# Low bits of float64 weights taken by a rounding on ScalarE, the sign as a halfword, one integer step per tile

## The chip, the core and the metric

The kernel runs on one core of a Trainium2 chip. Its engines work side by side, each through its own list of instructions in order: TensorE (PE in the profile, its weight loads PEld), VectorE (DVE), ScalarE (ACT), GpSimd (POOL), and SyncE (SP), which issues the transfers. The metric is the device time of one execution in microseconds, lower is better.

## What is computed

Three blocks follow each other: an attention with a pooled and a local part, a dense feed-forward block, and a block with eight experts. The change touches only how the weights of the middle block are made.

```python
h = x @ w_in                                   # x: 2304 x 512, w_in: 512 x 2048
g = np.where(pos, h, np.where(neg, 0.0, (h + beta) ** 2 / (4.0 * beta)))
return g @ w_out                               # w_out: 2048 x 512
```

`w_in` and `w_out` are float64. On the chip each double is two 32-bit words, the low word `lw` (even places) and the high word `hw` (odd places). To make a float32 of it, the kernel needs the sign, the exponent moved to float32's range, the 20 mantissa bits of `hw` moved up by three, and the three top bits of `lw` behind them.

## The kernel before

**Tiles.** `w_in` and `w_out` come as 16 tiles each of 128 x 512 doubles: 32 tiles, numbered by `f` (0 to 15) and `w` (1 for `w_in`, 0 for `w_out`). `feed` loads them in pairs into `RAW[w, f]` (named raw in the profile).

**One tile.** `prep(w, f)` takes a tile: `scale64` has ScalarE write `t = hw * 2^-111` read as float32 (`t<-raw`; in the first tiles the buffer is called gar), and then has GpSimd write `hw * 0` over `hw`, which leaves a signed zero (`raw<-raw`, POOL). VectorE then does two integer steps: `hw |= lw >> 29` (`raw<-raw`, DVE) and `t = (t << 3) | hw` (`t<-t,raw`). `parts` splits the result in a high part, a copy to fp32r on ScalarE (`wi<-t` or `wo<-t`), and a low part, the difference `t - hi`, on VectorE or GpSimd (also `wi<-t,wi` or `wo<-t,wo`). Tiles of `w_out` are also transposed on TensorE and multiplied with the gate's weights (`gate_rows`). A tile lands over the place of its raw form.

**Around it.** The first part of the program mixes four things: the attention of 16 pairs of heads (`pooled`, `local`), the 32 tiles, the load of its output in chunks of 256 rows (`load_chunks`, xio and xts), and the feed-forward block. That last one goes in steps: one step is 12 matmuls `xts,wi` (`gemm1`), a gate on ScalarE, VectorE and GpSimd (`gates`, gar, ghi, glo), and matmuls `wo,ghi` and `wo,glo`. There are 7 chunks of 16 steps, 112 in all, and the first 32 go through the two first chunks. A tile of number f is wanted by step f of the first chunk, so the first 32 steps follow the tiles. Until the first step TensorE fills its idle time with matmuls of an identity (`bk<-cst`).

**Order.** The program writes the order of every engine itself when it is built: each piece of work is a generator, `run` always takes the piece that could start first, with priorities (`PRIO`), and `spend` keeps the assumed time of each engine. A generator that yields a dict of two engines is put on that which would finish it first (`SUB` are the prices for the low part). So a change of one piece reorders everything beside it. The temporaries `TT` (`temps` holds the free ones) allow two tiles in work, and four early on. Line 128 issues all of ScalarE's work, line 141 that of VectorE and GpSimd, lines 120 and 124 that of TensorE, line 106 the transfers.

Of the kernel before, what the change touches and what calls it, by code (L numbers as in the profile page):

```python
# [11 lines left out]
F32 = mybir.dt.float32  # L12
F32R = mybir.dt.float32r
BF = mybir.dt.bfloat16
I32 = mybir.dt.int32
AF = mybir.ActivationFunctionType
OP = mybir.AluOpType
# [27 lines left out]
AI, AJ, AK = (-1,1,-1)  # L45
BACK = dict(V=0.0, G=1250.0, A=500.0)
SUB = (1600.0,1250.0)
DL = (300.0,2000.0)
RA, RB = (2,3)
GF = 565.0  # L50
# [42 lines left out]
def body(ctx, tc, qk_d, v4_d, vw_d, win, wout, wg, w1, w2, cst_d, bits_d, out):  # L93
# [4 lines left out]
    def spend(e, ns):  # L98

        at = max(free[e], cur[0] + (0.0 if cur[1] == e == "P" else 130.0 if cur[1] == e else 250.0))  # L100
        free[e] = cur[0] = at + ns
        cur[1] = e

    def dma(out, x):

        nc.sync.dma_start(out, x)  # L106
        free["D"] = max(free["D"], cur[0] + DL[0]) + 4.0 * int(np.prod(out.shape)) / 360.0
        return free["D"] + DL[1] - cur[0]

    def size(x):  # L110
        return int(np.prod(x.shape[1:]))
# [14 lines left out]
    def act(out, x, f, **kw):  # L126
        spend("A", {AF.Exp: 280.0, AF.Relu: 145.0}.get(f, 85.0) + 0.83 * size(x))
        return nc.scalar.activation(out, x, f, **kw)  # L128
# [15 lines left out]
    V = Engine("V", nc.vector, 65.0, 1.05)  # L144
    G = Engine("G", nc.gpsimd, 100.0, 2.3)
    ctx.enter_context(tc.manual_schedule())
    P = ctx.enter_context(tc.tile_pool(name="fixed", bufs=1))
# [17 lines left out]
    def f32(x):  # L165
        return x.bitcast(F32)
# [4 lines left out]
    WI, WO, RAW = {}, {}, {}  # L171

    def place(w, f, dt, name):
        return P.tile([128, 1024 if w else 1040], dt, name=nm(name), tag=f"w{w}_{f}", bufs=1)
# [3 lines left out]

    L = P.tile([128, NT, E], F32, name="L")
    w2g = P.tile([128, 16, 2, E], F32R, name="w2g")  # L180
    halfs = P.tile([128, 2], F32, name="halves")
    half, mhalf = halfs[:, 0:1], halfs[:, 1:2]
    V.memset(half, 0.5)
    V.memset(mhalf, -0.5)

# [3 lines left out]
    def words(w, f):  # L191
        return (RAW[w, f].rearrange("p (a b) -> p a b", b=2)[:, :, i] for i in range(2))
# [19 lines left out]
    def put(gen, at, e="N", got=None, last=""):  # L212
        seq[0] += 1
        late = RP if gen.__name__ in ("route", "index") and gen.gi_frame.f_locals["r"] == 1 else 0
        i = gen.gi_frame.f_locals.get("i", 9) if gen.__name__ in ("pooled", "local", "vsum") else 0
        queue[e].append((PRIO.get(gen.__name__, 2) + late + (0 if not i and gen.__name__ not in ("pooled", "local", "vsum") else (AK if gen.gi_frame.f_locals.get("g") else AI) if i < 4 else 0 if i < 8 else AJ), at, seq[0], gen, got, last))

    def spawn(gen, e="N", delay=0.0):
        put(gen, cur[0] + delay, e)
# [49 lines left out]
    def done(*k):  # L269
        return k[1] < 0 or k in flags  # L270

    def mark(*k):
        flags[k] = cur[0]
# [4 lines left out]
    def need(e, *names, cond=None, bank=0, temp=0):  # L278

        def f():  # L280
            few = [n for n in temps if n < (temp() if callable(temp) else temp)]
            if (cond and not cond()) or any(not room[n] for n in names) or len(open_banks()) < bank or (temp and not few):
                return None
            got = open_banks()
            got = got[:bank] if B0 else got[::-1][:bank]
            for b in got:
                banks.remove(b)
            return (got if bank > 1 else got[0] if bank else None, temps.pop(temps.index(max(few))) if temp else None,
                    *[room[n].pop(0) for n in names])
        f.engine = e  # L290
        return f
# [43 lines left out]
    def arrived(*k):  # L335
        mark(*k)
        yield "N"
# [17 lines left out]
    def feed():  # L355
        for j in range(16):
            for w in (1, 0):
                RAW[w, j] = place(w, j, I32, "raw")[:, 0:1024]
                n = dma(RAW[w, j], (win[:, j, :] if w else wout[j]).bitcast(I32))
                spawn(arrived("raw", j, w), "N", n)  # L360
# [140 lines left out]
    def scale64(w, f, t):  # L501
        _, hw = words(w, f)
        yield "A"
        act(t, f32(hw), AF.Copy, scale=2.0 ** -111)
        yield "G"
        G.tensor_scalar(f32(hw), f32(hw), 0.0, 1.0, op0=OP.mult, op1=OP.mult)
        mark("scaled", f, w)
        yield "N"

    def parts(w, f, x, n):  # L510
        (WI if w else WO)[f] = to = place(w, f, F32R, "wi" if w else "wo").rearrange("p (s c) -> p s c", s=2)
        hi, lo = (to[:, i, 0:512] for i in range(2))
        act(hi, x, AF.Copy)
        e = yield {"V": SUB[0], "G": SUB[1]}
        (G if e == "G" else V).tensor_tensor(lo, x, f32(hi), OP.subtract)
        mark("parts", f, w)
        if w:
            temps.append(n)
            mark("prep", f, 1)

    def prep(w, f):
        _, n = yield need("V", temp=lambda: 2 + MORE * (not done("av", FX, 0)), cond=lambda: done("raw", f, w) and done("begun", f - 1, w))
        mark("begun", f, w)
        t = TT[n]
        spawn(scale64(w, f, t))
        yield need("V", cond=lambda: done("scaled", f, w))
        ti = t.bitcast(I32)
        lw, hw = words(w, f)

        V.scalar_tensor_tensor(hw, lw, 29, hw, op0=OP.logical_shift_right, op1=OP.bitwise_or)  # L530
        V.scalar_tensor_tensor(ti, ti, 3, hw, op0=OP.logical_shift_left, op1=OP.bitwise_or)
        spawn(parts(w, f, t, n), "A")
        if w:
            return
        spawn(gate_rows(f, t))
        yield need("N", cond=lambda: done("parts", f, 0) and done("turned_rows", f))
        temps.append(n)
        mark("prep", f, 0)

    def gate_rows(f, x):  # L540

        b, _ = yield need("P", bank=1)
        ps = bank(b)
        for k in range(4):
            transpose(ps[:, 128 * k:128 * k + 128], x[:, 128 * k:128 * k + 128], ident)
        mark("turned_rows", f)
        _, _, kr = yield need("A", "rows")
        rows = at([128, 512], F32, f"rows{kr}")
        act(rows, ps, AF.Copy)
        drop(bank=b)  # L550
        b, _ = yield need("P", bank=1)
        pg = bank(b)[:, 0:E]
        for k in range(4):
            mm(pg, rows[:, 128 * k:128 * k + 128], wgk[:, k], start=k == 0, stop=k == 3)
        drop(rows=kr)
        yield need("A", cond=lambda: f in WO)

        to = WO[f][:, :, 512:520], w2g[:, f]
        for x in to:
            act(x[:, 0], pg, AF.Copy)  # L560
        yield "V"
        for x in to:
            V.tensor_tensor(x[:, 1], pg, f32(x[:, 0]), OP.subtract)
        drop(bank=b)
        mark("w2g", f)

    lw = []
# [238 lines left out]
    for f in range(16):  # L806
        put(prep(1, f), 0.0)
        put(prep(0, f), 0.0)
# [37 lines left out]

    cb = rt([128, 384], BF, "cb")
    tri_bf, low_bf, ones_bf = (cb[:, 128 * i:128 * i + 128] for i in range(3))
# [6 lines left out]
    V.memset(ones_bf, 1.0)  # L855
    bits = rt([128, NIT, 31], I32, "bits")
    dma(bits, bits_d)
# [3 lines left out]
    V.memset(openm, 1.0)  # L861
    first = rt([1, E], BF, "first")
    V.tensor_scalar(first, cst[0:1, C_E:C_E + E], 1.0 / 16, None, op0=OP.mult)
    tp = rt([128, NT, 2], BF, "tp")
    V.tensor_copy(tp[:, :, 0], cst[:, C_P:C_P + 1].to_broadcast([128, NT]))
    V.tensor_copy(tp[:, :, 1], cst[:, C_T:C_T + NT])
    low = rt([128, NT, 32], BF, "low")
    V.memset(low, 0.0)
# [6 lines left out]
    def kept(at, *shape):  # L875
        n = int(np.prod(shape))
        x = keep[:, at:at + n]
        return x if len(shape) == 1 else x.rearrange("p (a b) -> p a b", b=shape[1])
# [19 lines left out]
    def route(r):  # L898
        m = kept(18 * (r % 2), NT)
        bases = [keep[:, 36 + i:37 + i].bitcast(I32) for i in range(2)]  # L900
        V.tensor_reduce(m, L, AX.X, OP.max)
        Ah = rt([128, NT, E], BF, "A")
        oh = kept(90 + 8 * (r % 2), E)
        base = None
        for it, (sh, nj) in enumerate(STEPS if r < E - 1 else ()):
            if it == 0:
                thr = bits[:, 0, 0:nj]
            else:
                thr = rt([128, 31], I32, "thr", 1)[:, 0:nj]
                V.tensor_tensor(thr, pre, ni.to_broadcast([128, nj]), OP.bitwise_xor)  # L910
            C = rt([128, NT, 31], BF, "C", 1)
            V.tensor_tensor(C[:, :, 0:nj], m[:, :, None].to_broadcast([128, NT, nj]),
# [445 lines left out]
```

## Time and profile before

| what | us |
|---|---|
| median of 3 runs | 899.41 (894.22 to 908.81) |
| the profiled execution: device time | 900.66 |
| its span, first to last instruction | 898.5 |
| busy in the span: PE / DVE / ACT / POOL | 858.7 / 514.9 / 463.1 / 439.2 |
| first matmul of the first step | 61.8 |
| last issue of a weight tile's integer steps | 204.7 |

In the rows below, a stretch is given in us from the span's start. A row of the grouped view names line, engine, operation, out<-in, the shape of output and input, how many there are, the busy time in us and the mean in ns of one, and behind the second bar the idle time of the engine just ahead of them, with what ended it. Busy time of PE is no measure of its load, since its matmuls overlap.

### The profile page before, as it was taken

What the parts mean: (1) busy time and instruction counts of PE and PEld (TensorE: products, weight loads), DVE (VectorE), ACT (ScalarE), POOL (GpSimd) and SP (SyncE); (2) the same over time, 40 slices, a digit from 0 to 9 for tenths busy, and PEclk for the clock granted to TensorE, in tenths of its full rate; (3) what the DMA queues carried; (4) which work ended last, traced back from release to release, by engine and by line L of the source; (5) the groups of instructions that cost most, each with busy time, mean ns of one, the idle gap of its engine ahead of it and who ended that gap; (6) DMA issues with size and microseconds to landing.
All of it is one profiled execution on the core that took longest, in us unless ns stands there. A gap on an engine that the chain in (4) does not pass through costs nothing.

```text
span 898.5 us, 20588 instructions
## 1 busy us (share of the span) xinstructions
PE 858.7 (96%) x7891; PEld 777.8 (87%) x7891; DVE 514.9 (57%) x1469; ACT 463.1 (52%) x1295; POOL 439.2 (49%) x498
## 2 busy tenths in 40 slices
PE   7879999989899999999999999998999999999995
PEld 6768888878899999999999877777988998989995
DVE  6788989876454543423221564475576766767520
ACT  5877786776466666544444551032343443544641
POOL 3765477654244544444444210033855756657741
PEclk9999999999899999999999999997999999999998
DMA  9755455223222310301000000053433544436620
GB/s 308 232 176 185 139 179 194 88 61 111 89 64 70 103 42 15 95 1 49 1 25 1 30 1 6 1 207 126 145 122 128 183 140 152 150 101 209 208 84 27
DMA packets 39010, 95.41 MB, mean 106 GB/s; under 512 B 4992, under 2 KB 17152, under 8 KB 38912
## 3 DMA queue, kind: packets, MB, share of 16 engines
q1 hardware_dynamic: 35840, 84.66, 28.8%
q0 software_dynamic: 3072, 9.44, 3.4%
q8 instruction: 62, 1.02, 0.5%
q14 instruction: 36, 0.29, 0.1%
HBM read 79.92 MB, written 14.16 MB: 105 GB/s over the span
## 4 chain that ended last, share of the span: by engine, by line
PE 72%; DVE 8%; DMA 7%; issue 5%; ACT 4%; POOL 2%; SPq 1%; POOLq 0%; DVEq 0%; ACTq 0%
PE bk L120 70%; PE bk L124 3%; DMA stg<-in_w_dram 2%; DVE gar L141 1%; DMA vw<-in_vw_dram 1%; ACT gar L128 1%; DVE raw L141 1%; DMA v<-in_v_dram 1%; DMA x_rows<-xio 1%; POOL wo L141 1%; DMA x_cols<-x 1%; POOL out_dram L1116 1%; SPq L106 1%; DVE t L141 1%; DMA xg<-x_rows,idx 1%
## 5 line engine op out<-in xcount | busy, mean ns | idle before, releaser
L120 PE MATMUL bk<-xts,wi 128*128 128x256 f32 x1344 | 184.8, 288 | 5.3 <-ACT gar L128 3.7
L120 PEld LDWEIGHTS bk<-xts,wi 128*128 128x128 f32 x1344 | 170.6, 192 | 9.4 <-ACT gar L128 5.1
L120 PE MATMUL bk<-wo,ghi 128*128 128x256 f32 (+2 forms) x768 | 161.8, 309 | 0.0
L128 ACT ACTIVATE gar<-bk,halves 128x256 f32<-128x256 f32 x224 | 93.8, 471 | 91.0 <-PE bk L120 85.4
L141 DVE SCALAR_TENSOR_TENSOR gar<-gar 128x256 f32<-128x256 f32 x112 | 57.4, 513 | 115.7 <-ACT gar L128 115.4
L120 PEld LDWEIGHTS bk<-wo,ghi 128*128 128x128 f32 x768 | 115.9, 190 | 4.6 <-issue 0.4
L141 POOL TENSOR_TENSOR glo<-gar,ghi 128x256 fp32r<-128x256 f32 x86 | 65.8, 771 | 86.4 <-ACT ghi L128 71.5
L141 POOL TENSOR_TENSOR wi<-stg,wi 128x512 fp32r<-128x512 f32 x51 | 64.7, 1297 | 69.4 <-DMA stg<-in_w_dram 43.0
L120 PE MATMUL bk<-wo,glo 128*128 128x256 f32 (+2 forms) x384 | 90.3, 303 | 0.2 <-DVE glo L141 0.2
L141 POOL TENSOR_TENSOR gar<-gar 128x256 f32<-128x256 f32 x64 | 49.6, 775 | 72.4 <-DVE gar L141 47.0
L141 POOL TENSOR_TENSOR wo<-stg,wo 128x512 fp32r<-128x512 f32 x50 | 65.6, 1335 | 37.6 <-ACT wo L128 37.3
L120 PEld LDWEIGHTS bk<-wo,glo 128*128 128x128 f32 x384 | 62.1, 189 | 3.6 <-DVE glo L141 0.9
L128 ACT ACTIVATE ghi<-gar 128x256 fp32r<-128x256 f32 x112 | 46.7, 417 | 34.9 <-POOL gar L141 19.5
L120 PE MATMUL bk<-xT,wi 128*128 128x288 f32 x384 | 60.8, 311 | 0.1
L120 PE MATMUL bk<-hT,wi 128*128 128x288 f32 x384 | 60.5, 304 | 0.0
L128 ACT ACTIVATE wi<-stg 128x1024 fp32r<-128x1024 f32 x32 | 33.6, 1056 | 51.4 <-DMA stg<-in_w_dram 51.4
L120 PE MATMUL bk<-hT,wo 128*128 128x288 f32 x384 | 58.8, 302 | 0.0
L120 PE MATMUL bk<-xT,wo 128*128 128x288 f32 x384 | 58.4, 302 | 0.1
L128 ACT ACTIVATE lt<-lt,lmx 128x64 f32<-128x64 f32 x160 | 53.8, 342 | 8.9 <-DVE lmx L141 8.7
L120 PEld LDWEIGHTS bk<-xT,wi 128*128 128x128 f32 x384 | 54.4, 197 | 0.8 <-DVE xT L141 0.3
L120 PEld LDWEIGHTS bk<-xT,wo 128*128 128x128 f32 x384 | 52.0, 188 | 1.0 <-DVE xT L141 0.6
L120 PEld LDWEIGHTS bk<-hT,wi 128*128 128x128 f32 x384 | 52.1, 188 | 0.7
(189 smaller groups left out, 1669.2 us busy)
## 6 DMA issues: line engine op xcount, KB each, us to landing
stg<-in_w_dram SPq DMA_DIRECT2D x64, 512.0 KB
qk<-in_qk_dram SPq DMA_DIRECT2D x14, 590.0 KB
raw<-in_win_dram SPq DMA_DIRECT2D x16, 512.0 KB
raw<-in_wout_dram SPq DMA_DIRECT2D x16, 512.0 KB
v<-in_v_dram SPq DMA_DIRECT2D x32, 144.0 KB
xio<-x_cols SPq DMA_DIRECT2D x7, 512.0 KB
x_rows<-xio SPq DMA_DIRECT2D x7, 512.0 KB
vw<-in_vw_dram SPq DMA_DIRECT2D x16, 192.0 KB
```

The lines of the kernel that those rows point to most:

```text
L106: nc.sync.dma_start(out, x)
L120: return nc.tensor.matmul(out, w, x, **kw)
L124: return nc.tensor.transpose(out, x, i)
L128: return nc.scalar.activation(out, x, f, **kw)
L141: return fn(out, *args, **kw)
L1116: return nc.gpsimd.indirect_dma_start(**kw)
```

## The change

ScalarE gets one more instruction per tile ahead of `t = hw * 2^-111`. It reads the top byte of `lw` as an unsigned byte, scales it by 1/32, adds -31/64 from a one-column tile, cuts it at zero and rounds it to a 16-bit whole number, which is the top three bits of `lw`; it is written over the low halfword of `lw`. GpSimd's signed zero is no longer written over `hw` but as a bfloat16 over the high halfword of `lw`, so that `lw` then holds sign and low bits. VectorE's first integer step is gone; the second one takes `lw`. And the copy to the high part may now go to ScalarE or VectorE, as the builder's prices `HI` decide.

```diff
+HI = (630.0,900.0)
@@
-    halfs = P.tile([128, 2], F32, name="halves")
-    half, mhalf = halfs[:, 0:1], halfs[:, 1:2]
+    halfs = P.tile([128, 3], F32, name="halves")
+    half, mhalf, less = (halfs[:, i:i + 1] for i in range(3))
+    V.memset(less, -31.0 / 64)
@@ def scale64(w, f, t):
+        act(RAW[w, f].bitcast(U16).rearrange("p (a b) -> p a b", b=4)[:, :, 0],
+            RAW[w, f].bitcast(U8).rearrange("p (a b) -> p a b", b=8)[:, :, 3], AF.Relu, bias=less, scale=1.0 / 32)
         act(t, f32(hw), AF.Copy, scale=2.0 ** -111)
         yield "G"
-        G.tensor_scalar(f32(hw), f32(hw), 0.0, 1.0, op0=OP.mult, op1=OP.mult)
+        G.tensor_scalar(RAW[w, f].bitcast(BF).rearrange("p (a b) -> p a b", b=4)[:, :, 1], f32(hw), 0.0, 1.0, op0=OP.mult, op1=OP.mult)
@@ def parts(w, f, x, n):
-        act(hi, x, AF.Copy)
+        e = yield {"A": HI[0], "V": HI[1]}
+        if e == "A":
+            act(hi, x, AF.Copy)
+        else:
+            V.tensor_copy(hi, x)
@@ def prep(w, f):
-        V.scalar_tensor_tensor(hw, lw, 29, hw, op0=OP.logical_shift_right, op1=OP.bitwise_or)
-        V.scalar_tensor_tensor(ti, ti, 3, hw, op0=OP.logical_shift_left, op1=OP.bitwise_or)
-        spawn(parts(w, f, t, n), "A")
+        V.scalar_tensor_tensor(ti, ti, 3, lw, op0=OP.logical_shift_left, op1=OP.bitwise_or)
+        spawn(parts(w, f, t, n))
```

VectorE's list at two weight tiles in the early middle of the first part, before the change (raw is a tile's raw form, t a temporary, gar and glo belong to the gate, x to the attention):

```order
L141 SCALAR_TENSOR_TENSOR raw_265<-raw_265 128x512
L141 SCALAR_TENSOR_TENSOR t_69<-t_69,raw_265 128x512
L141 SCALAR_TENSOR_TENSOR gar_1021<-gar_1021 128x256
L141 TENSOR_SCALAR lsm_902<-lsm_902 128x6
L141 RECIPROCAL lsm_902<-lsm_902 128x6
L141 TENSOR_TENSOR gar_1021<-gar_1021 128x256
L141 TENSOR_TENSOR wo_1054<-t_70,wo_1054 128x512
```

Each tile has a `raw<-raw` step and a `t<-t,raw` step in a row; the subtraction `wo<-t,wo` that follows belongs to another tile, whose high part ScalarE has written in between.

VectorE's list at two tiles in the same part with the change:

```order
L144 SCALAR_TENSOR_TENSOR t_71<-t_71,raw_259 128x512
L144 CAST wi_894<-t_71 128x512
L144 TENSOR_TENSOR wi_894<-t_71,wi_894 128x512
L144 TENSOR_TENSOR wo_823<-bk_888,wo_823 128x8
L144 TENSOR_TENSOR w2g<-bk_888,w2g 128x8
L144 SCALAR_TENSOR_TENSOR t_70<-t_70,raw_261 128x512
L144 CAST wo_923<-t_70 128x512
```

The `raw<-raw` step is gone, and the copy to the high part (CAST) stands behind the step that is left, on the same engine. In the whole program 29 of the 32 copies are now there and 3 on ScalarE; 16 of the low parts are VectorE's (13 before), and 28 of the gate's `glo` (26 before).

ScalarE's list in the same part, before the change (rows, paT, laT, lt, pe and po belong to the attention and to the gate's weights):

```order
L128 ACTIVATE t_69<-raw_248 128x512
L128 ACTIVATE paT_696<-bk_760 72x288
L128 ACTIVATE pe_780,psm_718<-bk_692,pmx_717 96x144 x3
L128 ACTIVATE lt_0162_773,lsm_777<-lt_0162_773,lmx_776 128x64 x2
L128 ACTIVATE laT_814<-bk_785 128x256
L128 ACTIVATE lt_0162_773,lsm_777<-lt_0162_773,lmx_776 128x64 x2
L128 ACTIVATE wo_837<-t_70 128x512
```

And with the change:

```order
L131 ACTIVATE rows_824<-bk_809 128x512
L131 ACTIVATE raw_259<-raw_259,halves 128x512
L131 ACTIVATE t_71<-raw_259 128x512
L131 ACTIVATE po_859<-bk_830 128x144
L131 ACTIVATE wo_764<-bk_850 128x8
L131 ACTIVATE w2g<-bk_850 128x8
L131 ACTIVATE rows_872<-bk_863 128x512
```

The new `raw<-raw,halves` stands directly ahead of `t<-raw`, and the copy `wo<-t` of 512 columns is gone from the list here.

TensorE's list at the first step of the feed-forward block, before the change:

```order
L120 MATMUL bk_911<-wgk_84,rows_905 128x8 x4
L124 MATMUL bk_922<-cst,lt_0162_773 128x128 x2
L124 MATMUL bk_926<-cst,pe_780 72x96 x3
L120 MATMUL bk_941<-xts_895,wi_422 128x256 x12
L120 MATMUL bk_965<-laT_939,vw_791 64x58 x6
```

And with the change:

```order
L123 MATMUL bk_1143<-qk_481 64x64
L123 MATMUL bk_1153<-xts_1036,wi_256 128x256 x12
L127 MATMUL bk_1195<-cst,t_70 128x128 x4
L123 MATMUL bk_1153<-xts_1036,wi_420 128x256 x12
L127 MATMUL bk_1226<-cst,lt_0211_1012 128x128 x3
L123 MATMUL bk_1232<-wgk_85,rows_1223 128x8 x4
L123 MATMUL bk_1153<-xts_1036,wi_756 128x256 x12
```

More of the attention and more weight tiles now stand ahead of the first step: 338 matmuls other than fillers where there were 269 and, on VectorE ahead of the first low part of a chunk, 12 integer steps, 11 copies and 7 subtractions of tiles where there were 14 integer steps and 4 subtractions. From step 53 of the 112 on TensorE's list is the same as before, and so are the ends of the other lists.

## Rows read from the trace of the kernel before

**Rows 1.** Busy time by stretch: engine busy us (instructions), granted clock, DMA share, GB/s.

```profile
core 0: us, PE busy (x) PEld busy (x) DVE busy (x) ACT busy (x) POOL busy (x), PEclk, DMA share, GB/s
0.00:61.80 61.80, 49.29 (x627) 43.65 (x628) 44.32 (x98) 42.85 (x175) 35.72 (x52) 1.00 0.78 253
61.80:206.00 144.20, 136.10 (x1268) 118.10 (x1266) 125.62 (x239) 106.26 (x361) 89.36 (x100) 0.95 0.43 139
206.00:304.00 98.00, 94.44 (x961) 87.77 (x961) 50.92 (x130) 59.87 (x220) 40.19 (x55) 0.97 0.27 89
304.00:898.00 594.00, 578.88 (x5041) 528.30 (x5039) 294.05 (x1004) 254.16 (x542) 273.96 (x293) 0.99 0.27 86
```

**Rows 2.** Grouped view of VectorE, 0 to 206 us, shapes apart.

```profile
L141 DVE SCALAR_TENSOR_TENSOR raw<-raw 128x512 int32<-128x512 int32 x32 | 29.3, 916 | 5.0 <-POOL raw L141 5.0
L141 DVE SCALAR_TENSOR_TENSOR t<-t,raw 128x512 int32<-128x512 int32 x29 | 25.4, 876 | 2.2
L141 DVE SCALAR_TENSOR_TENSOR gar<-gar 128x256 f32<-128x256 f32 x29 | 19.1, 660 | 3.9 <-ACT gar L128 3.8
L141 DVE TENSOR_TENSOR glo<-gar,ghi 128x256 fp32r<-128x256 f32 x14 | 10.2, 729 | 1.6 <-ACT ghi L128 1.5
L141 DVE TENSOR_TENSOR wi<-t,wi 128x512 fp32r<-128x512 f32 x7 | 5.8, 823 | 0.8 <-ACT wi L128 0.7
L141 DVE TENSOR_TENSOR wo<-t,wo 128x512 fp32r<-128x512 f32 x4 | 4.0, 1001 | 1.4 <-ACT wo L128 1.4
```

**Rows 3.** Instructions of tiles raw and t: ns min/median/max, first and last start.

```profile
L141 DVE SCALAR_TENSOR_TENSOR raw<-raw x32: 665/694/1797, 16.8 to 203.7; 128x512 int32<-128x512 int32 x32
L141 POOL TENSOR_SCALAR raw<-raw x32: 640/665/1099, 15.1 to 201.7; 128x512 f32<-128x512 f32 x32
...
L141 DVE CAST cb<-t x1: 295/295/295, 546.3 to 546.3; 128x256 bf16<-128x256 f32 x1
```

**Rows 4.** Grouped view of ScalarE, 0 to 206 us, shapes apart.

```profile
L128 ACT ACTIVATE gar<-bk,halves 128x256 f32<-128x256 f32 x60 | 24.9, 468 | 12.5 <-PE bk L120 11.4 <-DVE glo L141 0.8 <-POOL lt L141 0.3
L128 ACT ACTIVATE t<-raw 128x512 f32<-128x512 f32 x29 | 19.2, 674 | 0.1
L128 ACT ACTIVATE ghi<-gar 128x256 fp32r<-128x256 f32 x28 | 11.7, 417 | 8.3 <-DVE gar L141 6.4 <-POOL gar L141 1.6
L128 ACT ACTIVATE wo<-t 128x512 fp32r<-128x512 f32 x15 | 9.5, 633 | 6.7 <-DVE t L141 6.6
L128 ACT ACTIVATE wi<-t 128x512 fp32r<-128x512 f32 x14 | 8.8, 631 | 4.0 <-DVE t L141 4.0
```

**Rows 5.** Grouped view of GpSimd, 0 to 206 us, shapes apart.

```profile
L141 POOL TENSOR_SCALAR raw<-raw 128x512 f32<-128x512 f32 x32 | 23.6, 744 | 7.1 <-ACT t L128 5.7 <-DMA qk<-in_qk_dram 1.1 <-ACT gar L128 0.2
L141 POOL TENSOR_TENSOR wo<-t,wo 128x512 fp32r<-128x512 f32 x10 | 15.2, 1515 | 10.9 <-ACT wo L128 9.5 <-PE bk L124 1.3
L141 POOL TENSOR_TENSOR glo<-gar,ghi 128x256 fp32r<-128x256 f32 x14 | 11.2, 796 | 13.6 <-ACT ghi L128 12.0 <-POOL raw L141 0.9 <-POOL lt L141 0.7
L141 POOL TENSOR_TENSOR wi<-t,wi 128x512 fp32r<-128x512 f32 x7 | 9.8, 1398 | 3.3 <-ACT wi L128 3.3
```

**Rows 6.** Grouped view of VectorE, 400 to 592 us.

```profile
L141 DVE SCALAR_TENSOR_TENSOR gar<-gar 128x256 f32<-128x256 f32 x32 | 13.6, 425 | 68.5 <-ACT gar L128 68.5
```

**Rows 7.** Instructions of tile wi alone by stretch; the columns are those of Rows 1.

```profile
61.80:206.00 144.20, 52.74 (x360) 48.45 (x360) 5.08 (x6) 7.59 (x12) 9.78 (x7) 0.95 0.43 139
304.00:356.00 52.00, 22.68 (x168) 20.67 (x168) 0.00 (x0) 0.00 (x0) 0.00 (x0) 1.00 0.11 33
400.00:500.00 100.00, 56.32 (x404) 51.79 (x404) 0.69 (x1) 0.63 (x1) 0.00 (x0) 1.00 0.05 17
```

More of the change, by code (lines that the diff above doesn't have):

```diff
@@ L14 @@
 BF = mybir.dt.bfloat16
+U16 = mybir.dt.uint16
+U8 = mybir.dt.uint8
 I32 = mybir.dt.int32
@@ L527, in prep @@
         ti = t.bitcast(I32)
-        lw, hw = words(w, f)
-        V.scalar_tensor_tensor(hw, lw, 29, hw, op0=OP.logical_shift_right, op1=OP.bitwise_or)
-        V.scalar_tensor_tensor(ti, ti, 3, hw, op0=OP.logical_shift_left, op1=OP.bitwise_or)
-        spawn(parts(w, f, t, n), "A")
+        lw, _ = words(w, f)
+        V.scalar_tensor_tensor(ti, ti, 3, lw, op0=OP.logical_shift_left, op1=OP.bitwise_or)
+        spawn(parts(w, f, t, n))
         if w:
```

## The prediction

> **What bounds the kernel now.** I read the busy time by stretch first, to find where the change can act at all. The orders of both programs agree from step 53 of the feed-forward block on, and that step starts at 304 us, so what lies behind it, 594 us, is the same work in the same order [rows 1]; a gain or a loss must come out of the first 304 us and is then carried to the end. Of these, the stretch from 206 us on is TensorE's: it runs 961 matmuls in 98.0 us, 0.102 us each, while VectorE and ScalarE are half idle [rows 1]. The stretch from the first step at 61.8 us to 206 us, where the last weight tile goes through, is the one that the change is in: VectorE is busy for 125.6 of 144.2 us (87%), ScalarE for 106.3 (74%), GpSimd for 89.4 (62%), and TensorE gets only 360 of the steps' matmuls done, 2.5 a us, where it does 4.0 a us later with no attention or tile beside them and 3.2 with attention alone [rows 1, 7]. So this stretch waits for the tiles and the attention, and the engine that is nearest to full is VectorE. The first 61.8 us have VectorE busy for 44.3 and ScalarE for 42.9 us [rows 1]; transfers share in their pace.
>
> The grouped views then show what VectorE does. The step that goes away is its largest group, 32 of 0.916 us; the one that stays costs 0.876 [rows 2]. Half of the first kind took 0.694 us or less [rows 3], so the mean holds 0.22 us of something that comes and goes. The gate's step shows the same: 0.660 us up to 206 us, 0.425 us between 400 and 592 us [rows 2, 6].
>
> **The change, part by part.** *VectorE.* Removed: 32 x 0.916 = 29.3 us. Added: 29 copies to the high part, an operation that the trace has not at this size. Its nearest row is the one CAST from a temporary, 256 columns in 0.295 us [rows 3]; 512 columns can't be under that, and they shouldn't be over the two-input step of the same size, 0.876 us [rows 2]. I take twice the row, 0.59 us, since a part of 0.295 is fixed and doubling it leaves room for the waits of this stretch: 29 x 0.59 = 17.1 us, with 8.6 and 25.4 as the ends. Three more low parts come to VectorE at 0.86 us (the mean over the two rows) for 2.6 us, and two more `glo` at 0.729 for 1.5 us [rows 2]. The sum is -29.3 + 17.1 + 2.6 + 1.5 = -8.1 us, between -16.6 and +0.2.
>
> The Trainium skill (VectorE: DVE Perf Modes, the perf-mode tier table) has a float32 copy between two SBUF tiles run at twice the rate of a two-input operation, 1227 ns for 2048 elements at two elements a cycle of 0.96 GHz; I estimate 0.427 us for 512 from it (1227 ns less 1536 elements at that rate), by which the sum would be -12.8 us and the time 887.9 us. No run here shows that at 512 columns.
>
> *ScalarE.* Added: 32 of the new rounding, which reads bytes eight apart and writes halfwords eight bytes apart. The nearest row is `t<-raw`, which reads every second word, 0.674 us; a cut at zero with a bias tile costs 0.468 where a plain copy costs 0.417, 0.051 more [rows 4]. So 0.725 us, 23.2 us in all; the ends are 0.674 (bytes and bias for nothing) and twice the 256-column form, 0.936. Removed: 29 copies of 0.632 us, 18.3 us [rows 4]. Net +4.9 us, between +3.2 and +11.6. What hides it: ScalarE is idle for 57 of the first 206 us [rows 1], and 10.6 us of that were waits for VectorE's `t` ahead of just these copies [rows 4]. Without that cover, the 4.9 us would stand in the tile's own chain.
>
> *GpSimd.* The 32 signed zeros stay; that they are written as halfwords I cost at nothing, since the reads and their number are the same, with 0.640 and 1.099 us as ends for 0.744 [rows 3, 5], -3.3 to +11.4 us, under the 80 us that GpSimd is idle up to 206 us [rows 1]. Three low parts (about 1.47) and two `glo` (0.796) go away: -6.0 us [rows 5].
>
> *Chain and order.* A tile's chain loses a step of 0.916 us and a change of engine, since the copy now stands behind the last integer step on the same engine, and gains 0.725 us ahead. What is queued behind the copy on VectorE is the next attention or gate step, which now waits 0.59 us more there but had waited 0.916 us for the step that is gone. The memset of one column costs nothing at the start, where VectorE is idle anyway. The order moves more than the operations: five more integer steps of tiles and 69 more matmuls stand ahead of the first step. Before it VectorE has -2 x 0.9 + 11 x 0.59 + 3 x 0.86 = 7.3 us more; since it is busy for 44.3 of 61.8 us there, that would make the first step about 10 us later if it keeps that share. In exchange 20 tiles are left behind the first step and not 25, so I let the two cancel.
>
> **Sum.** VectorE is the fullest engine where the tiles are made, so its saving counts one for one, and ScalarE's and GpSimd's changes lie in their idle time: 900.7 (device time of the profiled execution) - 8.1 = 892.6 us. The profiled execution is 1.3 us over the median of the runs shown, 0.1%, so it may stand for them; the runs themselves lie 1.6% apart.
>
> **The rivals.**
>
> *Port (no change).* The copy is made dearer by GpSimd, as the two-input steps are. GpSimd is busy for 125.1 of the first 206 us and an instruction of it takes 125.1/152 = 0.82 us [rows 1]. If the copy ends at the 0.876 us of the two-input step, VectorE gains nothing (+0.2), and half of ScalarE's 4.9 us shows: 900.7 + 0.2 + 2.5 = 903 us. For it speaks the spread of the removed step, 0.694 in the median to 1.797 [rows 3], and the gate's step that is dearer by 0.235 us in just this stretch [rows 2, 6]. Against it: even then the step that was removed had paid the same toll. The Trainium skill (SBUF — State Buffer, Who interferes with whom) has a rule for it: a copy on VectorE between SBUF tiles takes a port pair that GpSimd shares, and whoever comes first holds it for a whole instruction, while ScalarE never waits so. By that rule, moving the copy from ScalarE to VectorE buys a wait, and the trace agrees in so far as ScalarE's 512-column copies took 0.63 us on average [rows 4] and VectorE's two-input steps anything up to 1.8 [rows 3].
>
> *Late start (slower).* The first step comes late and is not caught up. ScalarE has, ahead of it, 12 roundings (8.7 us), five more `t<-raw` (3.4), six fewer copies (-3.8) and some 5 us more of attention and gate rows, 13 us, and at its share of 42.9 in 61.8 us that is 19 us. TensorE's 69 matmuls that are then done (two records each at up to 0.114 us, most of them small, half of it taken) are worth 8 us. If TensorE can't run denser afterwards than it did, the time is 900.7 + 19 - 8 = 912 us. It decides if the first step starts later than about 80 us; over 87 us it would be slower by more than 2%. Against it: TensorE has room, since up to 206 us it does 2.5 step matmuls a us and later 3.2 with attention beside them [rows 7].
>
> *Gap closes (faster).* With five tiles more ahead of the first step and a shorter chain, TensorE finds its tiles ready. At the 0.102 us per matmul that it keeps between 206 and 304 us, its 1268 matmuls up to 206 us would take 129 and not 144 us, 15 us less [rows 1]; with half of VectorE's 8.1 us ahead of the first step on top, 19 us: 881.5 us. Against it: the attention and the gate fill VectorE whatever the tiles cost.
>
> **Chances.** The forecast 892.6 us gets 0.50; the port rival 0.20; late start 0.14; gap closes 0.16. Two per cent of 899.4 us, about what a measurement of this kernel can tell from no change, is 18 us: faster means under 881.4, slower over 917.4 us. The gap rival sits on the first bound, so I put half of it below, and 0.07 of the forecast's own lower end (-16.6 us and a little of the gap): 0.15. Of late start I put 0.08 above 917.4, and 0.77 is left for no change. The range reaches from 879 to 910 us: below it lies a third of the gap rival and little else, above it most of the late start. The forecast's own range, by the bounds on VectorE alone, is 884 to 901 us.
>
> **What would show it.** In the profile after: the copies on VectorE near 0.59 us (under 0.45 the sum is better by over 4 us, at 0.85 the port rival holds); the rounding near 0.725 us on ScalarE; GpSimd's signed zero still near 0.744; VectorE's busy time up to the last tile lower by about 8 us; the first step at 62 to 75 us; step 53 at about 296 us; and from there to the end the same 594 us. It is wrong if step 53 comes no earlier with VectorE's time down by 8 us, which would mean that another engine, or the order, sets the pace of the tiles; or if what lies behind step 53 changes.

## The result and the profile after

The changed kernel took 912.5 us (median of 4 runs, 909.59 to 913.28) where the kernel before took 898.85 us beside it (4 runs): a ratio of 1.0139, 95% interval 1.0107 to 1.0170. It is slower by 1.4%, inside the 2% that count as no change, but 20 us from the 892.6 us forecast, on the other side, and past the upper end of the range. The profiled execution has a span of 911.1 us.

Busy time by stretch of the changed kernel, with the columns of [rows 1]; step 53 of the feed-forward block starts at 313.3 us:

```profile
0.00:61.80 61.80, 51.32 (x572) 45.41 (x572) 43.68 (x85) 47.85 (x161) 39.39 (x51) 0.94 0.73 248
61.80:206.00 144.20, 131.26 (x1188) 115.44 (x1189) 116.17 (x240) 113.21 (x334) 88.80 (x83) 0.92 0.38 125
206.00:304.00 98.00, 97.69 (x1069) 90.27 (x1068) 52.48 (x131) 64.30 (x236) 43.71 (x62) 1.00 0.29 94
0.00:313.30 313.30, 289.57 (x2909) 260.09 (x2909) 217.11 (x468) 232.31 (x757) 176.60 (x200) 0.95 0.42 140
```

And the kernel before up to its own step 53, which is the stretch to compare the last line with:

```profile
0.00:303.90 303.90, 279.73 (x2851) 249.42 (x2852) 220.87 (x465) 208.87 (x754) 165.23 (x205) 0.97 0.45 146
```

Up to 206 us VectorE looks 10 us less busy than in [rows 1]. That flatters the change, since its work is merely later: up to step 53, where both programs have done the same work, VectorE's saving is 220.9 - 217.1 = 3.8 us, ScalarE has 23.4 and GpSimd 11.4 us more. Step 53 comes 9.4 us later, and 597.8 us follow it (594.6 before).

The grouped view of the change, shapes apart, in which the weight tiles' own instructions stand:

```profile
L131 ACT ACTIVATE raw<-raw,halves 128x512 uint16<-128x512 uint8 x32 | 46.5, 1452 | 0.1
L144 POOL TENSOR_SCALAR raw<-raw 128x512 bf16<-128x512 f32 x32 | 45.1, 1426 | 21.2 <-ACT raw L131 21.1
L144 DVE SCALAR_TENSOR_TENSOR t<-t,raw 128x512 int32<-128x512 int32 x28 | 25.0, 892 | 3.1 <-POOL raw L144 2.5 <-DMA v<-in_v_dram 0.2
L144 DVE CAST wi<-t 128x512 fp32r<-128x512 f32 x13 | 9.3, 714 | 0.1
L144 DVE CAST wo<-t 128x512 fp32r<-128x512 f32 x12 | 6.1, 509 | 0.1
L144 DVE TENSOR_TENSOR wo<-t,wo 128x512 fp32r<-128x512 f32 x7 | 9.4, 1340 | 0.1
L144 DVE TENSOR_TENSOR wi<-t,wi 128x512 fp32r<-128x512 f32 x8 | 7.1, 882 | 0.2
```

The first two lines are the surprise. The rounding on ScalarE takes 1.452 us and not 0.725, and the signed zero on GpSimd, with as many elements read and written as before, 1.426 us and not the 0.744 of [rows 5]. GpSimd now waits 21.1 us for ScalarE's `raw`, the rounding; before it waited 5.7 us for ScalarE's `t` [rows 5]. (The signed zero no longer overwrites what `t` is made of, so it can run beside that step: 19 of the 32 start before it ends.)

Instructions of single tiles in the change (ns min/median/max):

```profile
L144 POOL TENSOR_SCALAR raw<-raw x32: 1315/1350/1864, 15.8 to 192.7; 128x512 bf16<-128x512 f32 x32
L144 DVE SCALAR_TENSOR_TENSOR t<-t,raw x28: 674/691/2244, 29.1 to 194.4; 128x512 int32<-128x512 int32 x28
L144 DVE CAST wi<-t x13: 396/427/1451, 36.3 to 192.0; 128x512 fp32r<-128x512 f32 x13
```

Even GpSimd's fastest signed zero, 1.315 us, is twice the 0.665 us of the median before [rows 3]. VectorE's step still takes 0.691 us in the median, but one took 2.244.

### The profile page after: what moved, and what is told of

Same layout as the page of the kernel before. It is cut to its first block, busy times and chain, and to the rows that moved or that the text cites. A ratio compares the mean times of both kernels' runs of the same rounds, so it can differ in the third digit from the quotient of the medians.

```text
span 911.1 us, 20695 instructions
## 1 busy us (share of the span) xinstructions
PE 868.6 (95%) x7947; PEld 788.6 (87%) x7947; DVE 513.8 (56%) x1472; ACT 486.5 (53%) x1298; POOL 450.0 (49%) x493
## 4 chain that ended last, share of the span: by engine, by line
PE 70%; issue 7%; ACT 6%; DVE 6%; DMA 5%; POOL 5%; SPq 0%; POOLq 0%; ACTq 0%; DVEq 0%
PE bk L123 66%; PE bk L127 3%; DMA stg<-in_w_dram 3%; POOL wi L144 1%; POOL wo L144 1%; ACT gar L131 1%; ACT lt L131 1%; ACT raw L131 1%; DVE wi L144 1%; DVE t L144 1%; DMA x_rows<-xio 1%; POOL out_dram L1126 1%; POOL raw L144 1%; DVE gar L144 1%; DMA v<-in_v_dram 1%
## 5 line engine op out<-in xcount | busy, mean ns | idle before, releaser
L123 PE MATMUL bk<-xts,wi 128*128 128x256 f32 x1344 | 181.8, 285 | 5.3 <-ACT gar L131 5.2
L123 PEld LDWEIGHTS bk<-xts,wi 128*128 128x128 f32 x1344 | 167.9, 189 | 9.7 <-ACT gar L131 7.7
L131 ACT ACTIVATE ghi<-gar 128x256 fp32r<-128x256 f32 x112 | 46.7, 417 | 33.2 <-POOL gar L144 18.6
L144 POOL TENSOR_SCALAR raw<-raw 128x512 bf16<-128x512 f32 x32 | 45.1, 1426 | 21.2 <-ACT raw L131 21.1
```

The source lines that it names most:

```text
L123: return nc.tensor.matmul(out, w, x, **kw)
L144: return fn(out, *args, **kw)
```

## The experiments

Three questions were open: whether it is the halfword form that makes the two instructions long, whether their length makes the kernel slow or the late first step and the new order do, and why time on GpSimd, an engine with 80 us of idle time, should count at all.

### Whole words instead of halfwords, in the same order

The builder prices an instruction by its operation, so three kernels could be made whose lists on every engine are those of the change and whose only difference is the form of the two instructions. They leave low bits of the weights out, so they tell of the time alone.

`e1_words`, both forms word-wide:

```diff
-        act(RAW[w, f].bitcast(U16).rearrange("p (a b) -> p a b", b=4)[:, :, 0],
-            RAW[w, f].bitcast(U8).rearrange("p (a b) -> p a b", b=8)[:, :, 3], AF.Relu, bias=less, scale=1.0 / 32)
+        act(f32(lw), f32(hw), AF.Relu, bias=less, scale=0.0)
-        G.tensor_scalar(RAW[w, f].bitcast(BF).rearrange("p (a b) -> p a b", b=4)[:, :, 1], f32(hw), 0.0, 1.0, ...)
+        G.tensor_scalar(f32(lw), f32(hw), 0.0, 1.0, op0=OP.mult, op1=OP.mult)
```

> Same order of every engine as the change, but the rounding on ScalarE and the signed zero on GpSimd work on whole words (the rounding reads hw and writes zeros over lw, so the three low bits are left out). Theory A (the two new forms cost twice what I took: 1.452 and 1.426 us in the changed kernel's profile): the rounding falls to about 0.72 us, the signed zero to about 0.74 us, the first step comes at 62 to 75 us and the time at 888 to 897 us. Theory B (the order with more attention and tiles ahead of the first step sets it, whatever the forms cost): the forms fall the same, but the first step stays later than 80 us and the time at 906 to 913 us.

Measured: ratio 0.9945 (0.9910 to 0.9980), so 5.0 us faster than the 902.34 us of before beside it. Busy time to its step 53, the grouped view to 206 us, and the tile t:

```profile
0.00:298.90 298.90, 282.85 (x2907) 255.59 (x2908) 207.86 (x468) 215.01 (x757) 157.21 (x200) 0.97 0.45 147
```

```profile
L131 ACT ACTIVATE raw<-raw,halves 128x512 f32<-128x512 f32 x32 | 24.6, 768 | 0.1
L144 POOL TENSOR_SCALAR raw<-raw 128x512 f32<-128x512 f32 x32 | 23.4, 738 | 14.7 <-ACT raw L131 14.6
L144 DVE SCALAR_TENSOR_TENSOR t<-t,raw 128x512 int32<-128x512 int32 x28 | 20.1, 718 | 2.5 <-POOL raw L144 2.5
```

```profile
L144 DVE SCALAR_TENSOR_TENSOR t<-t,raw x28: 677/682/1114, 28.9 to 179.9; 128x512 int32<-128x512 int32 x28
```

With nearly the durations that the prediction had assumed (0.768 and 0.738 us for 0.725 and 0.744), this order is a gain of 0.5%, and all of the change's loss lies in the two forms. The first step was expected at 62 to 75 us if the forms are to blame, and that missed: it starts at 82.1 us here too. So a start of that lateness belongs to the order and is caught up.

`e2_gp_word` has only GpSimd's edit of these two, `e3_act_word` only ScalarE's.

> Same order as the change; only the signed zero on GpSimd goes to a whole word (it overwrites the low bits, so these are left out), the rounding on ScalarE keeps its bytes and halfwords. Theory A1 (GpSimd's form is what counts, since each tile waits for it between ScalarE and VectorE): most of the loss goes, 895 to 901 us. Theory A2 (ScalarE's form is what counts, 46.5 us of it ahead of everything else that ScalarE does): 905 to 912 us. Theory B: no change from 912 us.

> Same order as the change; only the rounding on ScalarE goes to whole words (it writes zeros over lw, the low bits are left out), the signed zero on GpSimd keeps its halfword. Theory A1: little gained, 905 to 912 us. Theory A2: most of the loss goes, 895 to 901 us. Theory B: no change from 912 us.

Measured: `e2_gp_word` 0.9996 (0.9958 to 1.0033), `e3_act_word` 1.0099 (1.0064 to 1.0135). Up to step 53, first `e2_gp_word`, then `e3_act_word`:

```profile
0.00:306.20 306.20, 287.78 (x2909) 258.96 (x2909) 203.38 (x468) 231.02 (x757) 156.85 (x200) 0.96 0.45 143
```

```profile
0.00:312.00 312.00, 284.51 (x2907) 255.68 (x2908) 220.01 (x468) 215.54 (x757) 174.24 (x200) 0.97 0.44 141
```

The tile t of `e2_gp_word` and of `e3_act_word`:

```profile
L144 DVE SCALAR_TENSOR_TENSOR t<-t,raw x28: 675/684/1119, 29.6 to 187.5; 128x512 int32<-128x512 int32 x28
```

```profile
L144 DVE SCALAR_TENSOR_TENSOR t<-t,raw x28: 676/681/2253, 31.1 to 192.9; 128x512 int32<-128x512 int32 x28
```

The four kernels of one order close a square. GpSimd's halfword costs 1.5% (0.9945 to 1.0099) or 1.4% (0.9996 to 1.0139), whichever form the other engine has, and the intervals are apart both times. ScalarE's is smaller, 0.5% (0.9945 to 0.9996) or 0.4% (1.0099 to 1.0139); the intervals overlap both times, so a cost of it is likely and not shown. Each makes its own engine busier by 16 to 20 us up to step 53. The difference shows on VectorE: with GpSimd's halfword the same 468 instructions take 12 to 14 us more (220.0 for 207.9, 217.1 for 203.4), and the worst `t<-t,raw` goes from 1.1 to 2.25 us; with ScalarE's they take no more.

### The price of the forms by themselves

`f_forms` appends instructions of several forms behind the end of the change, three of each kind (45 in all), where no other work runs.

```diff
+    for o, x in ((d_h, s_b), (d_w, s_b), (d_h, s_w), (d_w, s_w), (d_h, s_h), (d_hd, s_b), (d_d, s_d), (d_h, s_u), ...):
+        for _ in range(3):
+            nc.scalar.activation(o, x, AF.Relu, bias=less, scale=1.0 / 32)
+    for o, x in ((d_hb, s_w), (d_w, s_w), (d_hbd, s_w), (d_hbd, s_d), (d_d, s_d)):
+        for _ in range(3):
+            nc.gpsimd.tensor_scalar(o, x, 0.0, 1.0, op0=OP.mult, op1=OP.mult)
+    for _ in range(3):
+        nc.vector.tensor_copy(f32(fdst[:, 0:512]).bitcast(F32R), f32(fsrc[:, 0:512]))
```

The first letter stands for source or destination; h is halfwords 8 bytes apart, hb the same as bfloat16, hd and hbd dense halfwords, w words 8 bytes apart, d dense words, b bytes 8 apart, u unsigned words 8 bytes apart.

> The changed kernel with 30 small instructions behind its end, alone on their engine: 512 columns on ScalarE in nine forms, on GpSimd in five, and the copy on VectorE. If the access by bytes or halfwords doubles the rounding, the word form should take 0.70 to 0.76 us and one of byte read and halfword write alone 1.4 us; if the conversion to whole numbers does it, the halfword written from words is dear as well. On GpSimd, if the halfword write eight bytes apart costs it, the dense bfloat16 write takes 0.74 us or less. The copy on VectorE should take about 0.43 us alone. The time itself should be some 25 us over the change's.

Its one run took 943.3 us, 31 us more than the change where some 25 were expected. Grouped view behind the end, the rounding's own form from 890 to 905 us and then ScalarE and VectorE from 905 us on:

```profile
L1332 ACT ACTIVATE stg<-stg,halves 128x512 uint16<-128x512 uint8 x3 | 4.3, 1427 | 2.0 <-DVE stg L1321 2.0
...
L1332 ACT ACTIVATE stg<-stg,halves 128x512 uint16<-128x512 f32 x3 | 4.3, 1422 | 0.1
L1332 ACT ACTIVATE stg<-stg,halves 128x512 uint16<-128x512 uint16 x3 | 4.3, 1422 | 0.1
L1332 ACT ACTIVATE stg<-stg,halves 128x512 uint16<-128x512 uint8 x3 | 2.2, 745 | 0.1
L1332 ACT ACTIVATE stg<-stg,halves 128x512 f32<-128x512 uint8 x3 | 2.2, 727 | 0.1
L1337 DVE CAST stg<-stg 128x512 fp32r<-128x512 f32 x3 | 1.3, 427 | 36.5 <-POOL stg L1335 36.4
```

The first three write halfwords 8 bytes apart (from bytes, words and halfwords), the fourth (from bytes) dense halfwords, the fifth words 8 bytes apart. Reading bytes costs nothing here (0.727 us); a dense halfword output costs almost nothing (0.745), and a word output 8 bytes apart nothing (0.727). Halfwords that are 8 bytes apart cost 1.42 us for 0.73, whatever is read. GpSimd, from 921.5 to 926 us (the halfwords 8 bytes apart) and from 928 to 931.9 (words, and dense halfwords):

```profile
L1335 POOL TENSOR_SCALAR stg<-stg 128x512 bf16<-128x512 f32 x3 | 4.0, 1323 | 20.3 <-ACT stg L1332 20.1
...
L1335 POOL TENSOR_SCALAR stg<-stg 128x512 f32<-128x512 f32 x3 | 1.9, 639 | 2.4 <-ACT stg L1332 2.2
L1335 POOL TENSOR_SCALAR stg<-stg 128x512 bf16<-128x512 f32 x3 | 1.9, 636 | 0.2
```

It is the same there: 1.323 for 0.636 us. Nothing else ran beside these, so the length is the instruction's own and no contention.

### Why GpSimd's time counts

`d1_write` and `d2_read` are `e1_words` with one more GpSimd instruction ahead of each sign: a fill that only writes, or the word-wide signed zero a second time, which reads as well.

```diff
+        nc.gpsimd.memset(f32(lw), 0.0)                                                       # d1_write
+        nc.gpsimd.tensor_scalar(f32(lw), f32(hw), 0.0, 1.0, op0=OP.mult, op1=OP.mult)        # d2_read
         G.tensor_scalar(f32(lw), f32(hw), 0.0, 1.0, op0=OP.mult, op1=OP.mult)
```

> Edit: e1_words, with one instruction more on GpSimd ahead of each sign: a fill with zeros of the words that the sign is then written to (128x512 words, written only, nothing read from SBUF). The order of everything else stays that of e1_words, which took 0.9945 of the time before; GpSimd's part for a tile should become about 0.5 us longer (estimate from the 0.738 us of the sign, which also reads), against 0.68 us in the change. Both whole-word steps leave the low bits of the weight out, as in e1_words. Theory A (GpSimd's own occupancy and the chain sign, then VectorE's step, carry the loss): time 903 to 909 us by before's 902, ratio 1.001 to 1.008. Theory B (GpSimd's reading and writing holds VectorE's two-input steps back, and only a step that reads does): ratio 0.993 to 0.999, VectorE's t<-t,raw mean stays at about 720 to 760 ns.

> Edit: e1_words, with the whole-word signed zero made twice on GpSimd, the second over the first: about 0.70 us more of GpSimd for a tile, the amount that the halfword form adds (1.426 against 0.738), with reading and writing of words as in the first. Order as in e1_words; the low bits of the weight are left out, as there. Theory A (GpSimd's occupancy and the chain): ratio 1.004 to 1.012, near e3_act_word, whose sign alone is the halfword form (1.0099), first GEMM step later than the 82.1 us of e1_words by several us. Theory B (interference with VectorE): ratio also 1.004 to 1.012, but with VectorE's t<-t,raw at 840 ns or more, and d1_write well below. Theory C (it is the scattered halfword write itself, not the length of the instruction): ratio stays at 0.993 to 0.999.

Measured: `d1_write` 1.0007 (0.9971 to 1.0044), `d2_read` 1.0070 (1.0044 to 1.0097), by 900.88 us of before beside them. Busy time to step 53 and the tile t, first of `d1_write`:

```profile
0.00:306.40 306.40, 289.28 (x2908) 260.95 (x2909) 206.67 (x468) 215.64 (x757) 172.70 (x232) 0.95 0.44 143
```

```profile
L144 DVE SCALAR_TENSOR_TENSOR t<-t,raw x28: 676/682/1221, 29.8 to 186.7; 128x512 int32<-128x512 int32 x28
```

and of `d2_read`:

```profile
0.00:311.00 311.00, 288.93 (x2909) 259.33 (x2909) 212.74 (x468) 215.48 (x757) 179.93 (x232) 0.96 0.43 141
```

```profile
L144 DVE SCALAR_TENSOR_TENSOR t<-t,raw x28: 673/693/1776, 30.2 to 192.2; 128x512 int32<-128x512 int32 x28
```

All six kernels of the one order, beside before, up to step 53 (us):

| kernel | step 53 | VectorE | ScalarE | GpSimd | ratio |
|---|---|---|---|---|---|
| before | 303.9 | 220.9 | 208.9 | 165.2 | 1 |
| both in words (`e1_words`) | 298.9 | 207.9 | 215.0 | 157.2 | 0.9945 |
| ScalarE's halfword (`e2_gp_word`) | 306.2 | 203.4 | 231.0 | 156.9 | 0.9996 |
| words, and a fill (`d1_write`) | 306.4 | 206.7 | 215.6 | 172.7 | 1.0007 |
| words, sign twice (`d2_read`) | 311.0 | 212.7 | 215.5 | 179.9 | 1.0070 |
| GpSimd's halfword (`e3_act_word`) | 312.0 | 220.0 | 215.5 | 174.2 | 1.0099 |
| the change | 313.3 | 217.1 | 232.3 | 176.6 | 1.0139 |

The first ratio falls between the ranges of the two theories, the second fits both, and both hold a part. A fill that leaves VectorE's time as it was (206.7 for 207.9) delays step 53 by 7.5 us for 15.5 us more of GpSimd, so GpSimd's own time counts, idle share or not. (In the times the fill is worth 0.6%, and the intervals of the two ratios overlap by 0.001.) How much comes through is no fixed share. 16.0 us more of ScalarE delay step 53 by 7.3 us with GpSimd's words (`e1_words` to `e2_gp_word`), and 16.8 us by only 1.3 us with its halfword (`e3_act_word` to the change). These are single profiled executions; the change's own program, profiled again at the head of `f_forms`, has step 53 at 311.9 us for 313.3.

A GpSimd instruction that reads adds a second loss: VectorE's two-input steps are held up. GpSimd's halfword, with about the fill's added time, costs 13.1 us by step 53, not 7.5, and VectorE is busy for 220.0 us and not 206.7. The longest `t<-t,raw` of `e3_act_word`, and what GpSimd did in that time (start and length in us):

```profile
169.56 2.25 DVE L144 SCALAR_TENSOR_TENSOR t<-t,raw 128x512 int32<-128x512 int32 x1 [0.19 <-POOL raw L144]
168.20 2.52 POOL L144 TENSOR_SCALAR raw<-raw 128x512 bf16<-128x512 f32 x2
170.53 0.74 POOL L144 TENSOR_TENSOR glo<-gar,ghi 128x256 fp32r<-128x256 f32 x1
```

The step starts inside a signed zero and ends 0.55 us after the gate's subtraction behind it. The longest one of `d2_read` (1.776 us) is not beside the doubled sign but beside a low part on GpSimd, and ends 0.55 us after that, too:

```profile
115.49 1.78 DVE L144 SCALAR_TENSOR_TENSOR t<-t,raw 128x512 int32<-128x512 int32 x1
115.32 1.40 POOL L144 TENSOR_TENSOR wo<-t,wo 128x512 fp32r<-128x512 f32 x1 [0.37 <-DVE wo L144]
```

So single longest steps don't tell what the sign costs; a count does. Up to step 53, take of each VectorE instruction with two inputs from SBUF what it took over the shortest of its form in the traces of this case, and put it down to the GpSimd instruction that it overlaps longest. Beside signed zeros that makes 6.4 us in `e1_words`, 11.4 in `d2_read`, 22.7 in `e3_act_word` and 18.4 in the change; beside the fill of `d1_write` 0.7 us, over 18 instructions; beside all other work of GpSimd it is 21.5 to 25.2 us in each of the six kernels of the one order. (In `d2_read` this loss can't be told from the length of the second sign by step 53 alone: GpSimd is busier by 22.7 us there, 7.2 more than with the fill.)

The Trainium skill (SBUF — State Buffer, Who interferes with whom) says that a VectorE instruction with two SBUF inputs contends with a GpSimd instruction that reads SBUF and not with one that only writes it. The traces agree: that count, and the mean of `t<-t,raw`, 0.718 us in `e1_words`, 0.743 in `d1_write`, 0.889 in `d2_read`.

### The copies, the order and the builder's prices

`p1_flex` is the kernel before with the change's `HI` alone (copies where the builder likes, 21 of 32 on VectorE), `p2_actcopy` is the change with all copies on ScalarE, `h1_prices` the change with the two instructions priced at what they take, and `c1_one_half` a version with one halfword instruction: GpSimd's signed zero over the whole `hw` as before, then ScalarE's rounding into the low half of it.

```diff
-        spawn(parts(w, f, t, n), "A")                                                   # p1_flex, on before
+        spawn(parts(w, f, t, n))
-        e = yield {"A": HI[0], "V": HI[1]}                                              # p2_actcopy, on the change
+        act(hi, x, AF.Copy)
+        spend("A", 1450.0)                       # h1_prices, on the change, ahead of the rounding
+        spend("G", 1400.0)                       # and ahead of the signed zero
+        G.tensor_scalar(f32(hw), f32(hw), 0.0, 1.0, op0=OP.mult, op1=OP.mult)           # c1_one_half
+        nc.scalar.activation(RAW[w, f].bitcast(U16).rearrange("p (a b) -> p a b", b=4)[:, :, 2], ...)
```

> The kernel before with one part of the change alone: the copy to the high part may go to ScalarE or VectorE by the prices HI; both integer steps and the word-wide signed zero stay. 21 of the 32 copies go to VectorE. If what was won in the run with whole words came from the copies (they follow the last integer step on the same engine), 893 to 899 us against some 900 of the kernel before. If a copy on VectorE is as dear as the trace of the change shows it in its mean (0.64 us, waiting for GpSimd), it only loads the fullest engine by 13 us: 902 to 910 us.

> The change without its other part: rounding and halfword sign stay, all 32 copies to the high part go back to ScalarE. Theory A1 (GpSimd's halfword write is what costs the time): as slow as the change or slower, since ScalarE then has the rounding's 46.5 us and the copies' 20 us: 912 to 925 us. If the copies on VectorE were what made the change slow: 898 to 906 us.

> The change with the builder's prices for the two new forms set to what they took, 1450 ns for the rounding (570 assumed) and 1400 ns for the signed zero (689 assumed), so that the order is planned with them; the instructions are the same but 32 copies and 24 low parts go to VectorE. If the order that was planned with wrong prices is what costs the time (Theory B), 895 to 903 us. If the forms themselves cost it (Theory A1), 906 to 914 us.

> A version that computes the same bits with one halfword write per tile and not two: GpSimd writes its signed zero over the whole word hw as the kernel before does (0.744 us), after ScalarE has read hw; then ScalarE's rounding goes into the low halfword of hw (1.45 us), and the integer step takes hw. Theory A1: near the run with GpSimd's whole word, 897 to 904 us. If the extra change of engine in each tile's chain weighs as much as GpSimd's halfword, 905 to 912 us.

Measured, by 904.72 us of before beside them:

| kernel | ratio | interval | first step | step 53 |
|---|---|---|---|---|
| `p1_flex` | 1.0091 | 1.0061 to 1.0121 | 64.4 | 308.6 |
| `p2_actcopy` | 1.0161 | 1.0135 to 1.0187 | 72.0 | 320.1 |
| `h1_prices` | 1.0146 | 1.0097 to 1.0195 | 66.2 | 315.3 |
| `c1_one_half` | 1.0184 | 1.0159 to 1.0209 | 65.8 | 319.3 |

Busy time to step 53 of `p1_flex` and then of `h1_prices`:

```profile
0.00:308.60 308.60, 283.63 (x2857) 252.38 (x2857) 233.74 (x487) 198.72 (x733) 168.31 (x204) 0.96 0.44 144
```

```profile
0.00:315.30 315.30, 284.51 (x2882) 252.19 (x2883) 215.36 (x473) 230.08 (x754) 172.19 (x198) 0.97 0.44 141
```

Moving copies to VectorE with nothing taken from it adds 12.9 us there (233.7 for 220.9, six more of the gate's `glo` among it) and costs 0.9%, as the second of its two expectations had it. Whether the move pays inside the change is not told: without it the ratio is 1.0161, and the interval overlaps the change's. `h1_prices` speaks against the late start too: priced truly, the builder starts the steps at 66.2 us, near the 61.8 us of before, and the kernel is as slow as the change.

`c1_one_half` missed both of its expectations, and is the slowest of all. Up to its step 53:

```profile
0.00:319.30 319.30, 284.68 (x2869) 253.74 (x2870) 200.95 (x464) 230.21 (x754) 157.64 (x207) 0.96 0.43 139
```

Its engines are as busy as in `e2_gp_word` (203.4, 231.0 and 156.9 us), which takes the time of before and has no halfword on GpSimd either. So the order and the tile's chain can cost as much as the forms did: here the sign stands ahead of ScalarE's long rounding. Its loss is not taken apart, and the square above shows the price of the forms for the change's own order alone.

## Why the prediction was wrong

*The rounding, 0.725 us between 0.674 and 0.936.* Wrong: 1.452. Its nearest row, `t<-raw`, differs from it in the reads (bytes for words) and the writes (halfwords 8 bytes apart for words), and the prediction looked at the reads. Bytes are free (0.727 us); the writes double it.

*The signed zero, which "I cost at nothing", between 0.640 and 1.099.* Wrong, and this is the step that cost most: "the reads and their number are the same" was true, and the instruction takes 1.426 us. In the same order it makes 1.4 to 1.5% of the time, 13 to 14 us, more than the whole forecast gain. The upper end came from an instruction of the old form that had been held up, so both ends were prices of words.

*ScalarE's and GpSimd's changes "lie in their idle time".* Wrong in kind. Their idle time up to 206 us, 57 and 80 us, is a sum over waits of a chain: rounding, sign (with `t` beside it), integer step, copy, subtraction, on three engines with few temporaries, and a step that grows delays those behind it. With 15.5 us more of GpSimd step 53 came 7.5 us later (`d1_write`), and with 16.0 us more of ScalarE 7.3 us (`e2_gp_word`), though 1.3 us where GpSimd's sign was long as well.

*VectorE, -8.1 us, and "its saving counts one for one".* The parts were fair, not the sum. (The mean of the two rows of low parts is 0.89 us and not 0.86, and the rival "gap closes" adds up to 881.7 us and not 881.5; neither matters.) Its largest group is gone. The 29 copies took 0.643 us on average for the 0.59 taken (18.6 us in all: 15.4 in the two rows above, and four more out of gar). The estimate from the Trainium skill (VectorE: DVE Perf Modes, the perf-mode tier table) was 0.427 us; that is exactly what an undisturbed copy takes, in the median of the change and behind the end in `f_forms`, and the mean is half as much again. But the low parts that came to VectorE cost more than 0.86 us (`wo<-t,wo` 1.340), and up to step 53 only 3.8 us were saved. With word-wide forms 13.0 us were saved there, with 6.1 us more on ScalarE and 8.0 less on GpSimd, and the time fell by 5: VectorE's saving did not count one for one, though it was the fullest engine.

*The first step at 62 to 75 us, "late start" as a rival.* The step came at 88.7 us, past the rival's point of decision, and the rival's 912 us is almost the time measured. Its mechanism is not what happened. `e1_words` starts at 82.1 and is faster than before, `e2_gp_word` at 86.5 and takes the same, `h1_prices` at 66.2 and is as slow as the change. More tiles done ahead of the first step are repaid after it, as the prediction's main line had it. A rival's right time is no proof of its story.

*The port rival.* It was thought of for the copy, whose mean is 0.22 us over its undisturbed 0.427, but the two-input steps pay more once GpSimd's signed zero is long. The prediction said that the removed step "had paid the same toll"; in the change the one that was left paid as much as before (0.892 us for 0.876), where word-wide forms would have brought it to 0.718.

*The tail.* 597.8 us for 594.6. The six kernels of the one order have 592.3 to 599.4, in no order that fits their times. The feed-forward block is not where they part: the first matmul of the experts (`xT,wi`) comes 311.9 to 313.9 us behind step 53 in all of them and in before, and the last stretch then takes 279.9 to 286.8 us. Why that varies stays open; it blurs what is read from a single execution's end (`e1_words` and `e2_gp_word` ended within 0.2 us of each other, with 7.3 us between their steps 53).

## What to carry to other kernels

Price an instruction by the width and the spacing of what it writes, not only by its element count: 512 halfwords 8 bytes apart cost double, and one tiny kernel tail with the form alone shows it. An engine's idle share does not by itself hide time in the middle of a chain that hops between engines; here up to half of it came through by step 53, and once almost none. And time on GpSimd can count beyond its own list where VectorE has two-input steps beside it: here a longer instruction that reads cost VectorE 12 to 14 us, and a fill that only writes cost it nothing.

## What the runs showed of the hardware that was not expected

Writing 512 halfwords a partition 8 bytes apart took 1.42 us on ScalarE and 1.32 on GpSimd with nothing else running (`f_forms`); dense halfwords took 0.745 and 0.636, words 8 bytes apart 0.727 and 0.639. Whether it is the spacing or the part of a word that doubles it was not tried at other spacings.

The granted clock of TensorE was low ahead of the first step. The change from 60 to 80 us, in the columns of [rows 1]:

```profile
60.00:80.00 20.00, 16.43 (x143) 14.83 (x141) 12.56 (x28) 11.83 (x36) 10.29 (x10) 0.56 0.43 145
```

That is mostly the lower level, 1.2 GHz (0.50); before and `e1_words` have 0.83 there, `d1_write` 0.50. In the change TensorE had waited 3.6 us for VectorE's x between 61.7 and 65.3 us. What the clock adds to the 1.4% was not separated, but it does not go with the time: `d1_write`, with the lowest clock of these there, takes the time of before, and `e3_act_word`, with 0.80, is 1.0% slower.
